# Output weights in rows of 3584 bytes, and the last sixteen value chunks summed and turned apart, in a one-core attention decode step

## The chip, the cores and the metric

The kernel runs on one core of one Trainium2 chip. The metric is device time in microseconds (us), from the start to the end of the program on that core; 653.36 us is the median of three runs before the change (653.25 to 653.43).

## What is computed

One token for each of four sequences (B = 4, D = 448) goes through a layer norm and then two branches. Branch A is attention over a cache; branch B is a small two-layer network with GELUs. The output adds their product to x.

```python
q = (xn @ wq).reshape(B, 1, 16, 256)              # 16 query heads of 256
k, v = repeat(k_cache, 2), repeat(v_cache, 2)     # 8 kv heads, 8192 positions, bf16
p = softmax(einsum("bhqd,bhkd->bhqk", q, k) / 16)
o = einsum("bhqk,bhkd->bhqd", p, v)
s = o.reshape(B, 1, 4096) @ wo                    # wo is [4096, 448]
out = x + s * silu(B(xn))                         # xn = layernorm(x)
```

The two caches are 128 MiB each. wq and wo are 3584 KB each; the other weights are smaller. Nearly all bytes are read once and used once.

## The kernel before

**Pairs.** The 32 (sequence, kv head) combinations are taken two at a time: 16 pairs, two neighbouring kv heads of one sequence. A pair's keys are two tiles of 4 MB (`kn`, one per kv head slot), its values 8 MB (`vb`). Partition p holds positions in chunks of 128 columns: `NC2` = 128 chunks of 128 positions for the pair, the upper 64 partitions for the second kv head.

**TensorE's program** (`prog_pe`) is written out by hand. `body` runs once for each pair. For every group of four key chunks it transposes eight 128x128 blocks (`f_t`, L655), VectorE and ScalarE copy them from PSUM to SBUF (`evac`, L350 and L352), and three groups later the score matmuls follow (`f_s`, L668). At the end of a pair, the value matmuls of the *pair before* stand between the last score groups (`f_pv`, L700): eight columns of probabilities `pT` are the weights, two value chunks (512 columns) stream through, and four matmuls write four groups of 32 PSUM partitions of `psv`. Then come the row maxima, a broadcast, and the exponentials on ScalarE (`exps`, L376).

**The turn.** `psv` holds sums by (group, chunk parity, head row) on partitions and by the 256 head columns along the free axis. VectorE copies it to `po` (`f_po`, L540). In the next pair's key stage `f_tr` (L693) multiplies `po`, every second column as weights, with a selector `sel`, in float32: this adds the groups up and puts head columns on the 128 partitions. VectorE multiplies with the reciprocal of the row sums into `OT_all` (`f_ot`, L543).

**After the last pair** `finish` does the rest: the turn of pair 14, the output matmuls of the heads whose wo rows are there early (`f_ou`, L736, four groups of 32 partitions, summed later by `selb` at L776), the values of pair 15 in pieces as they land, and the output matmuls of the other heads (`f_o`, L746, two halves of 224 columns side by side into `o_ps`). The pieces are bounded by `PIECES`. The last two (`ND = 2`) are not summed in `psv`: `f_direct` (L756) loads each chunk's every second column as weights and streams 32 columns of `pT` through, so that the result comes out turned at once in `ol_ps`; the turn of `po` (L783) is added into the same PSUM. VectorE's last `f_ot` writes pair 15's part of OT; after `f_o` it multiplies and adds (L590, L592), and two small stores end the program.

**Loads.** All large loads stand in SyncE's queue, in the order: wq, w3, keys of pair 0, w4, nine heads of wo (`dwo`), then keys of pair i and values of pair i-1 in turn, at the end the values of pair 15 in pieces into the key buffer (`dvl0` to `dvl4`), and last wo for heads 0 to 6 in four loads (`LATE`, `dwl0` to `dwl3`). Heads 0 to 6 come late because w4 lies in their place in `wo_sb` until the middle of the program (`v_w4`). A load into a used buffer waits for VectorE's release (`v_k`, `v_v`). A partition of a wo head holds two rows of 448: 1792 bytes in one run. `take` (L318) waits for a semaphore and takes its count off again.

Of the kernel before, what the change touches and what calls it, by code (L numbers as in the profile page):

```python
# [7 lines left out]
ALU = mybir.AluOpType  # L8
AX = mybir.AxisListType
F32 = dt.float32  # L10
BF16 = dt.bfloat16

P = 128
# [50 lines left out]
def bass_recurrent_scan__gqa_block_cached__mixer_s_mlp__decode_kernel(  # L64
# [13 lines left out]
    Bn, Sq, D = A_x.shape  # L78
    _, HKV, SK, DH = A_k_cache.shape
    HD = A_wq.shape[1]  # L80
    HQ = HD // DH
    REP = HQ // HKV
# [10 lines left out]
    NDG = 2  # L93
# [26 lines left out]
    PIECES = (0, 64, 96, 116, 124, NC2)  # L120
# [3 lines left out]
    ND = 2  # L124

    LATE = ((0, 1), (2, 3), (4, 5), (6,))
    NLATE = sum(len(g) for g in LATE)
# [16 lines left out]
    with ExitStack() as es:  # L144
        def sb(name, shape, dty):
            return es.enter_context(nc.sbuf_tensor(name, shape, dty))
# [5 lines left out]
        wo_sb = sb("wo_sb", [P, HQ, NHALF, D], BF16)  # L152
# [15 lines left out]
        po = sb("po", [P, CP * DH], F32)  # L168
        rmax = sb("rmax", [P, REP], F32)
# [42 lines left out]
        assert DK * HDH <= NCH * DH and NF <= NLATE * NHALF  # L212
# [13 lines left out]
        OT = OT_all[:, 2 * PW:].rearrange("p (b g d r) -> p g r d b", g=HKV, d=NHALF,  # L226
                                                 r=REP)
# [8 lines left out]
        def prog_sp(sp):  # L236
# [59 lines left out]
            wo_src = A_wo.rearrange("(h p c) n -> p h (c n)", p=P, c=NHALF)  # L296

            def load_wo(lo, hi, sem):
                sp.dma_start(wo_sb[:, lo:hi].rearrange("p h c n -> p h (c n)"),
                             wo_src[:, lo:hi]).then_inc(S[sem], 16)  # L300

            load_wo(NLATE, HQ, "dwo")
# [6 lines left out]
            for i, hs in enumerate(LATE):  # L309
                load_wo(hs[0], hs[-1] + 1, "dwl%d" % i)  # L310
# [6 lines left out]
        def take(eng, name, n=1):  # L317
            return eng.wait_ge(S[name], n).then_inc(S[name], -n)  # L318
# [75 lines left out]
        def prog_dve(v):  # L394
# [147 lines left out]
            def f_ot(at, src):  # L542
                return v.tensor_tensor(  # L543
                    OT_all[:, bass.ds(at, PW)].rearrange("p (s a r) -> p a s r", s=NS, a=NHALF),
                    src.rearrange("p a (s r) -> p a s r", s=NS),
                    rz[:, :].rearrange("p (s r) -> p s r", s=NS).unsqueeze(1).broadcast_to(
                        [P, NHALF, NS, REP]), ALU.mult)

            def turned(at):
                take(v, "p_m3")  # L550
                return f_ot(at, psm[:, P + 2 * NR:P + 2 * NR + NHALF * NR].rearrange(
                    "p (a n) -> p a n", a=NHALF))

            with nc.Fori(0, NH * TW, PW, engines=[mybir.EngineType.DVE]) as at:
# [32 lines left out]
            f_ot(NH * TW + PW, ol_ps[:, 0:NHALF * PVW].rearrange("p (a n) -> p a n", a=NHALF)[  # L587
                :, :, 0:NR]).then_inc(S["v_ot"], 1)
# [6 lines left out]
        def prog_pe(pe, xn_mark, xn2_mark):  # L595
# [91 lines left out]

            def f_tr():
                take(pe, "v_po")
                for dh in range(NHALF):  # L690
                    o = P + (2 + dh) * NR
                    for i in range(CP):
                        ins = pe.matmul(psm[:, o:o + NR], po[:, i * DH + dh:(i + 1) * DH:NHALF],  # L693
                                        sel[:, i, 0:NR], start=(i == 0), stop=(i == CP - 1))
                ins.then_inc(S["p_m3"], 1)
# [33 lines left out]
            ALONE = HQ - NS * REP  # L729

            def f_ou(hs):
                for hq in hs:
                    for dh in range(NHALF):
                        k = (hq - NLATE) * NHALF + dh
                        o = k % NCG * CGW
                        ins = pe.matmul(ou_ps[o:o + PQ, 0:D], OT[:, hq // REP, hq % REP, dh, :],  # L736
                                        wo_sb[:, hq, dh, :], start=(k < NCG),
                                        stop=(k >= (ALONE - NLATE) * NHALF - NCG))
                return ins


            def f_o(hs, stop=False):
                for hq in hs:
                    for dh in range(NHALF):
                        for i in range(NDG):
                            ins = pe.matmul(o_ps[i * PQ:(i + 1) * PQ, 0:DQ],  # L746
                                            OT[:, hq // REP, hq % REP, dh, :],
                                            wo_sb[:, hq, dh, i * DQ:(i + 1) * DQ], start=False,
                                            stop=stop and hq == hs[-1] and dh == NHALF - 1)
                return ins  # L750

            def f_direct(i):
                take(pe, "dvl%d" % i, 16)
                for dh in range(NHALF):
                    for kk in range(PIECES[i], PIECES[i + 1]):
                        ins = pe.matmul(ol_ps[:, dh * PVW:(dh + 1) * PVW], kv[:, kk, dh:DH:NHALF],  # L756
                                        pT[:, kk * NR:kk * NR + PVW],
                                        start=(dh == 0 and kk == PIECES[NPIECE - ND]),
                                        stop=(dh == NHALF - 1 and kk == NC2 - 1))
                return ins  # L760

            def finish():
                f_tr()
                take(pe, "dwo", 16)
                take(pe, "v_ot")
                f_ou(range(NLATE, ALONE)).then_inc(S["p_ou"], 1)
                take(pe, "a_exp")
                f_sum()
                pb = PIECES[NPIECE - ND]
                for i in range(NPIECE - ND):  # L770
                    take(pe, "dvl%d" % i, 16)
                    ins = f_pv(kv, PIECES[i], PIECES[i + 1], pb)
                    if i == 0:
                        take(pe, "v_a")
                        for n in range(NDG):
                            pe.matmul(o_ps[n * PQ:(n + 1) * PQ, 0:DQ], selb[:, :],  # L776
                                      ou_f[:, n * DQ:(n + 1) * DQ], start=True, stop=False)
                ins.then_inc(S["p_pv"], 1)
                f_direct(NPIECE - ND)
                take(pe, "v_po")  # L780
                for dh in range(NHALF):
                    for i in range(CP):
                        pe.matmul(ol_ps[:, dh * PVW:(dh + 1) * PVW],  # L783
                                  po[:, i * DH + dh:(i + 1) * DH:NHALF], sel[:, i, :],
                                  start=False, stop=False)
                f_direct(NPIECE - 1).then_inc(S["p_pv"], 1)
                take(pe, "dwl0", 16)
                f_o(LATE[0])
                take(pe, "v_ot")
                f_o(range(ALONE, HQ))  # L790
                for i in range(1, len(LATE)):
                    take(pe, "dwl%d" % i, 16)
                    ins = f_o(LATE[i], i == len(LATE) - 1)
                ins.then_inc(S["p_o"], 1)
# [65 lines left out]
```

## Time and profile before

| what | value |
|---|---|
| median of three runs | 653.36 us (653.25 to 653.43) |
| the profiled execution's own time | 652.84 us |
| its span, first to last instruction | 651.3 us |
| TensorE: matmul busy, weight load busy | 501.3 us (77%), 409.0 us (63%) |
| VectorE, ScalarE busy | 257.2 us (39%), 268.7 us (41%) |
| mean granted TensorE clock | 0.882 |
| DMA | 279.13 MB, mean 429 GB/s |
| DMA packets | 10642; 1029 under 512 bytes, 3081 under 2 KB |
| transposes of keys (L655) | 4096 matmuls, 301.6 us |
| the turn in `f_tr` (L693) | 136 passes, 258 ns each; loads of 128 columns in f32, 196 ns |
| wo matmuls at the end (L746) | 44, each 128x224, 267 ns |

PE is TensorE's matmuls, PEld its weight loads, which run beside them; a float32 matmul shows as two passes. "L318" is the line of the helper that waits for a semaphore, so a wait whose releaser is "PEq L318" is one on TensorE's own queue for some semaphore. "issue" is time for which the profile shows no cause. Times inside the span count from its start. Where the text names landings, it means the moment at which the last of the 16 DMA engines has counted up that load's semaphore.

### The profile page before, as it was taken

Reading aid. Unit: us, or ns where it says so; the run is one execution under the profiler, and the core shown is the slowest. Engines: PE = TensorE matmul, PEld = TensorE weight load, DVE = VectorE, ACT = ScalarE, POOL = GpSimd, SP = SyncE. Lnnn points to the kernel's source line nnn. Section 1 sums busy time; section 2 is a strip of 40 time slices with the busy share of each in tenths; the row PEclk is TensorE's granted clock in tenths of the full one; section 3 lists DMA queues with packets and bytes.
Section 4 is the critical chain, followed back from the end, with each engine's and each line's share of the span. In section 5 each row is a group of like instructions: output and inputs, shape, how many; then the busy total and the mean of one; then the engine's idle time right before and its main releaser. Section 6 shows DMA issues by size and latency. Waiting matters only on the chain. (4 is left out here: it accounts for less than half of the span.)

```text
span 651.3 us, 22030 instructions
## 1 busy us (share of the span) xinstructions
PE 501.3 (77%) x9695; PEld 409.0 (63%) x9695; DVE 257.2 (39%) x507; ACT 268.7 (41%) x361; POOL 3.7 (1%) x18
## 2 busy tenths in 40 slices
PE   2978979695876959589587967959597695959957
PEld 0976949384673938559286764928567393755924
DVE  7434525252452524335153442515245252433511
ACT  6644626063451615436144542606345161543600
POOL 2000000000000000000000000000000000000000
PEclk9989979697996969889788997969889797987968
DMA  9999999999999999999999999999999999999997
GB/s 382 436 419 436 431 437 447 421 441 429 442 443 407 455 415 447 423 431 459 411 452 415 455 423 429 441 427 443 425 445 435 417 449 421 445 425 429 455 406 305
DMA packets 10642, 279.13 MB, mean 429 GB/s; under 512 B 1029, under 2 KB 3081, under 8 KB 3593
## 3 DMA queue, kind: packets, MB, share of 16 engines
q1 hardware_dynamic: 10616, 278.99, 99.5%
q8 instruction: 7, 0.11, 0.1%
q14 instruction: 3, 0.02, 0.0%
q10 hardware_dynamic: 16, 0.01, 0.0%
HBM read 278.99 MB, written 0.00 MB: 428 GB/s over the span
## 5 line engine op out<-in xcount | busy, mean ns | idle before, releaser
L655 PE MATMUL pst<-ident_b,kn 128*128 128x128 bf16 x4096 | 301.6, 221 | 21.6 <-PEq L318 20.1
L352 ACT ACTIVATE kT<-pst 128x1024 bf16<-128x1024 bf16 x224 | 226.1, 1023 | 116.6 <-ACTq L318 116.2
L350 DVE COPY kT<-pst 128x1024 bf16<-128x1024 bf16 x288 | 197.5, 691 | 172.4 <-DVEq L318 172.4
L655 PEld LDWEIGHTS pst<-ident_b,kn 128*128 128x128 bf16 x4096 | 239.2, 99 | 23.5 <-issue 23.5
L700 PE MATMUL psv<-vb,pT 128*8 128x512 bf16 x1024 | 105.1, 506 | 99.6 <-PEq L318 98.7
L668 PE MATMUL psc<-qc,kT 128*128 128x4 bf16 x4096 | 174.2, 165 | 7.7 <-PEq L318 5.8
L668 PEld LDWEIGHTS psc<-qc,kT 128*128 128x128 bf16 x4096 | 153.4, 97 | 36.8 <-issue 36.5
L376 ACT ACTIVATE pT<-psc,negb 64x128 bf16<-64x128 f32 x64 | 28.4, 535 | 244.0 <-ACTq L318 243.8
L700 PEld LDWEIGHTS psv<-vb,pT 128*8 128x8 bf16 x1024 | 25.0, 94 | 133.2 <-issue 123.1
L511 DVE TENSOR_REDUCE rmax<-psc 64x2 f32<-64x256 f32 x32 | 13.5, 422 | 137.2 <-DVEq L318 137.0
L693 PE MATMUL psm<-sel,po 128*128 128x4 f32 x136 | 18.4, 258 | 1.4 <-PEq L318 1.4
L693 PEld LDWEIGHTS psm<-sel,po 128*128 128x128 f32 x136 | 17.3, 196 | 1.5 <-issue 1.5
L376 ACT ACTIVATION_READ_ACCUMULATOR pT<-psc,negb 64x1 f32 x64 | 16.4, 256 | 0.0
L540 DVE COPY po<-psv 128x512 f32<-128x512 f32 x17 | 11.7, 691 | 9.1 <-DVEq L318 9.1
L532 DVE COPY negb<-psm 128x4 f32<-128x4 f32 x16 | 2.6, 161 | 31.3 <-DVEq L318 31.3
L521 DVE TENSOR_REDUCE gmax<-psm 2x2 f32<-2x128 f32 x16 | 4.5, 279 | 21.2 <-DVEq L318 21.2
L364 ACT ACTIVATE vb<-pT 128x5000 bf16<-128x5000 bf16 (+2 forms) x3 | 10.6, 3568 | 0.1
L677 PEld LDWEIGHTS psm<-ident_f,rmax 128*2 128x2 f32 x16 | 1.3, 80 | 12.6 <-issue 12.6
L681 PEld LDWEIGHTS psm<-diag,ones_f 2*128 2x128 f32 x32 | 4.7, 182 | 7.0 <-issue 7.0
L600 PE MATMUL pst<-ident_b,xn_b 4*128 4x4 bf16 x14 | 0.7, 162 | 9.6 <-DVE xn_b L425 9.6
L600 PEld LDWEIGHTS pst<-ident_b,xn_b 4*128 4x128 bf16 x14 | 0.5, 100 | 10.5 <-issue 9.5
L685 PE MATMUL psw<-rowsum,ones_f 128*128 128x4 f32 x34 | 6.5, 263 | 0.0
(93 smaller groups left out, 86.4 us busy)
## 6 DMA issues: line engine op xcount, KB each, us to landing
kn<-in_A_k_cache_dram SPq DMA_DIRECT2D x30, 4096.0 KB, 26.5
kn<-in_A_k_cache_dram SPq DMA_DIRECT2D x4, 2048.0 KB, 16.7
vb<-in_A_v_cache_dram SPq DMA_DIRECT2D x2, 4096.0 KB, 23.1
kn<-in_A_v_cache_dram SPq DMA_DIRECT2D x1, 4096.0 KB, 27.7
vb<-in_A_wq_dram SPq DMA_DIRECT2D x1, 3584.0 KB, 11.4
kn<-in_A_v_cache_dram SPq DMA_DIRECT2D x1, 2048.0 KB, 26.2
wo_sb<-in_A_wo_dram SPq DMA_DIRECT2D x1, 2016.0 KB, 40.8
vb<-in_B_w_dram SPq DMA_DIRECT2D x1, 1568.0 KB, 14.1
```

The costliest lines, as they stand in the source:

```text
L350: engine.tensor_copy(dst, src).then_inc(S["v_ev"], 1)
L352: engine.activation(dst, src, ACT.Copy).then_inc(S["a_ev"], 1)
L364: f = act.activation(t, pT[:, 0:1].broadcast_to([P, t.shape[1]]), ACT.Copy)
L376: ins = act.activation(pT[own, 0:NC2 * NR].rearrange("p (c n) -> p n c", n=NR)[:, n], psc[own, 0:NC2 * NR].rearrange("p (c n) -> p n c", n ...
L511: ins = v.tensor_reduce(rmax[own, :], psc[own, 0:NC2 * NR].rearrange("p (c n) -> p n c", n=NR)[:, t * REP:(t + 1) * REP], AX.X, ALU.max)
L540: v.tensor_copy(po[:, :], psv[:, 0:CP * DH]).then_inc(S["v_po"], 1)
L655: ins = pe.transpose(dst[:, n * P:(n + 1) * P], kn[:, t, GC * j + kl, half * P:(half + 1) * P], ident_b[:, :])
L668: ins = pe.matmul(psc[:, kk * NR:(kk + 1) * NR], kT[:, j % RING, n * P:(n + 1) * P], qc[:, :, half, :], start=(half == 0), stop=(half == N ...
L681: pe.matmul(psm[:, P:P + NR], ones_f[0:REP, :], diag[:, :], start=True, stop=True).then_inc(S["p_m2"], 1)
L685: pe.matmul(psw[:, 0:NR], ones_f[:, :], rowsum[:, :], start=True, stop=True).then_inc(S["p_s"], 1)
L693: ins = pe.matmul(psm[:, o:o + NR], po[:, i * DH + dh:(i + 1) * DH:NHALF], sel[:, i, 0:NR], start=(i == 0), stop=(i == CP - 1))
L700: ins = pe.matmul(psv[o:o + CP * NR, 0:CP * DH], pT[:, kk * NR:(kk + CP) * NR], src[:, kk:kk + CP, :].rearrange("p c d -> p (c d)"), start ...
```

## The change

wo is laid out by kv head instead of by query head. A partition of a kv head's tile now holds four rows of wo, 3584 bytes in one run; the lower 64 partitions belong to the first query head of the kv head, the upper 64 to the second, and a partition's rows are four neighbouring columns of that head (`NDC` = 4). So the turn has to put every fourth head column on a partition, for each query head on its own half: `turn_out` makes four column steps x two halves, with 64 columns of weights each. `f_ot` runs once for each half. The first wo load has four kv heads (eight query heads), the late ones three whole kv heads and the fourth in two halves. The last three pieces of values (112 to 128, sixteen chunks) no longer go through `f_direct`: `f_end` sums them like the others but one chunk at a time, into `psc`; VectorE copies them to a new tile `pb`, and `pb` is turned after `po`, into the same PSUM. Output matmuls of late groups 0 and 1 now stand ahead of the wait for pair 15's OT (before: heads 0 and 1 alone).

```diff
-    PIECES = (0, 64, 96, 116, 124, NC2)
+    PIECES = (0, 64, 96, 112, 120, 124, NC2)
-    ND = 2
-    LATE = ((0, 1), (2, 3), (4, 5), (6,))
+    ND = 3
+    NDC = REP * NHALF
+    LATE = ((0, 0, NDC), (1, 0, NDC), (2, 0, NDC), (3, 0, NDC // 2), (3, NDC // 2, NDC))
...
-        wo_sb = sb("wo_sb", [P, HQ, NHALF, D], BF16)
+        wo_sb = sb("wo_sb", [P, HKV, NDC, D], BF16)
+        pb = sb("pb", [P, DH], F32)
...
-            wo_src = A_wo.rearrange("(h p c) n -> p h (c n)", p=P, c=NHALF)
-            load_wo(NLATE, HQ, "dwo")
+            wo_src = A_wo.rearrange("(g p c) n -> p g c n", p=P, c=NDC)
+            sp.dma_start(wo_sb[:, NLATE:].rearrange("p g c n -> p g (c n)"),
+                         wo_src[:, NLATE:].rearrange("p g c n -> p g (c n)")
+                         ).then_inc(S["dwo"], 16)
...
-            for i, hs in enumerate(LATE):
-                load_wo(hs[0], hs[-1] + 1, "dwl%d" % i)
+            for i, (g, lo, hi) in enumerate(LATE):
+                sp.dma_start(wo_sb[:, g, lo:hi].rearrange("p c n -> p (c n)"),
+                             wo_src[:, g, lo:hi].rearrange("p c n -> p (c n)")
+                             ).then_inc(S["dwl%d" % i], 16)
...
             def f_ot(at, src):
-                return v.tensor_tensor(
-                    OT_all[:, bass.ds(at, PW)].rearrange("p (s a r) -> p a s r", s=NS, a=NHALF),
...
+                for r in range(REP):
+                    own = slice(r * P // REP, (r + 1) * P // REP)
+                    ins = v.tensor_tensor(
+                        OT_all[own, bass.ds(at, PW)].rearrange("p (s c) -> p s c", s=NS),
+                        src[own].rearrange("p c (s r) -> p r s c", s=NS)[:, r],
+                        rz[own, :].rearrange("p (s r) -> p r s", s=NS)[:, r].unsqueeze(2)
+                        .broadcast_to([P // REP, NS, NDC]), ALU.mult)
+                return ins
...
             take(v, "p_pv")
             f_po()
             take(v, "p_pv")
+            v.tensor_copy(pb[:, :], psc[:, 0:DH]).then_inc(S["v_po"], 1)
+            take(v, "p_pv")
+            f_ot(NH * TW + PW, ol_ps[:, 0:NDC * NR].rearrange("p (c n) -> p c n", c=NDC)).then_inc(S["v_ot"], 1)
...
+            def turn_out(dst, src, n, start, stop):
+                for c in range(NDC):
+                    for i in range(n):
+                        for r in range(REP):
+                            own = slice(r * P // REP, (r + 1) * P // REP)
+                            ins = pe.matmul(dst[own, c * NR:(c + 1) * NR],
+                                            src[:, i * DH + c:(i + 1) * DH:NDC], sel[:, i, 0:NR],
+                                            start=start(c, i), stop=stop(c, i))
+                return ins
...
-            def f_direct(i):
+            def f_end(i):
                 take(pe, "dvl%d" % i, 16)
-                for dh in range(NHALF):
-                    for kk in range(PIECES[i], PIECES[i + 1]):
-                        ins = pe.matmul(ol_ps[:, dh * PVW:(dh + 1) * PVW], kv[:, kk, dh:DH:NHALF],
-                                        pT[:, kk * NR:kk * NR + PVW],
...
+                for kk in range(PIECES[i], PIECES[i + 1]):
+                    o = kk % NCG * CGW
+                    ins = pe.matmul(psc[o:o + NR, 0:DH], pT[:, kk * NR:(kk + 1) * NR], kv[:, kk, :],
+                                    start=(kk < PIECES[NPIECE - ND] + NCG), stop=(kk >= NC2 - NCG))
                 return ins
...
                 ins.then_inc(S["p_pv"], 1)
-                f_direct(NPIECE - ND)
+                f_end(NPIECE - ND)
                 take(pe, "v_po")
-                for dh in range(NHALF):
-                    for i in range(CP):
-                        pe.matmul(ol_ps[:, dh * PVW:(dh + 1) * PVW],
-                                  po[:, i * DH + dh:(i + 1) * DH:NHALF], sel[:, i, :],
-                                  start=False, stop=False)
-                f_direct(NPIECE - 1).then_inc(S["p_pv"], 1)
-                take(pe, "dwl0", 16)
-                f_o(LATE[0])
+                turn_out(ol_ps, po, CP, lambda c, i: c == 0 and i == 0, lambda c, i: False)
+                for i in range(NPIECE - ND + 1, NPIECE):
+                    ins = f_end(i)
+                ins.then_inc(S["p_pv"], 1)
+                take(pe, "v_po")
+                turn_out(ol_ps, pb, 1, lambda c, i: False, lambda c, i: c == NDC - 1
+                         ).then_inc(S["p_pv"], 1)
+                last = len(LATE) - 1
+                for i in range(2):
+                    take(pe, "dwl%d" % i, 16)
+                    f_o(*LATE[i])
                 take(pe, "v_ot")
-                f_o(range(ALONE, HQ))
-                for i in range(1, len(LATE)):
+                for g in range(ALONE, HKV):
+                    f_o(g, 0, NDC)
+                for i in range(2, len(LATE)):
                     take(pe, "dwl%d" % i, 16)
-                    ins = f_o(LATE[i], i == len(LATE) - 1)
+                    ins = f_o(*LATE[i], stop=i == last)
                 ins.then_inc(S["p_o"], 1)
```

`f_tr` calls `turn_out` as well, so the turn in every pair's key stage has the new form. The line numbers of the kernel after differ: the turn is L699, `f_o` L754, `f_end` L763.

## The prediction

> **What bounds the kernel now.** I read the page's slices and queues first, then the chain that ended last, then the last microseconds in order of time, then the DMA issues. Slices and queue (each DMA digit is the busy share of 16 engines in tenths):
>
> ```profile
> PEclk9989979697996969889788997969889797987968
> DMA  9999999999999999999999999999999999999997
> GB/s 382 436 419 436 431 437 447 421 441 429 442 443 407 455 415 447 423 431 459 411 452 415 455 423 429 441 427 443 425 445 435 417 449 421 445 425 429 455 406 305
> ...
> q1 hardware_dynamic: 10616, 278.99, 99.5%
> ```
>
> One queue moves 279 MB without a hole. The landing marks say the same: every 4 MB takes 9.65 to 9.71 us (two exceptions of 9.84 and 9.95), that is 433.7 GB/s. The issues are far ahead: the last value pieces and the wo loads stand 25 to 28 us in the queue before they land, so no issue and no buffer release is late.
>
> ```profile
> 647.95 0.04 issue
> 647.99 0.98 PE pst L746 x12
> 649.00 0.40 DVE res L590
> 649.42 0.38 DVE out_b L592
> ```
>
> This is the chain of waits (start, length, what). It begins where TensorE waits for the third late wo load. The order of time (start, length, engine, line, idle before), and then the issues of late wo (KB each, us from issue to landing):
>
> ```profile
> 643.65 0.69 DVE L540 COPY po<-psv 128x512 f32<-128x512 f32 x1 [5.26 <-DVEq L318]
> 644.46 1.02 PEld L783 LDWEIGHTS pst<-sel,po 128*128 128x128 f32 x8
> 645.71 1.90 PE L746 MATMUL pst<-wo_sb,OT_all 128*32 128x224 bf16 x32
> 647.96 0.78 PEld L746 LDWEIGHTS pst<-wo_sb,OT_all 128*32 128x32 bf16 x12 [0.57 <-issue]
> ```
>
> ```profile
> wo_sb<-in_A_wo_dram SPq DMA_DIRECT2D x3, 448.0 KB, 27.1
> wo_sb<-in_A_wo_dram SPq DMA_DIRECT2D x1, 224.0 KB, 16.7
> ```
>
> The last load lands at 648.41, its four matmuls end at 648.96, VectorE and the store take the rest to 651.3. So the end is the DMA stream plus 2.9 us. But TensorE idles only 0.57 us between 645.7 and 648.96: it is a close second.
>
> Landings of the tail before: value pieces 634.63, 639.50, 642.55, 643.80, 644.45; late wo 645.58, 646.71, 647.86, 648.41.
>
> [...]448 KB of wo takes 1.13 us, where its bytes at 433.7 GB/s take 1.06. [...] The f32 loads of 128 columns start 117.5 ns apart (L783)[...]. [...]637.1 to 640.5 ran at clock 0.50. [...]at L736 four loads of 32 columns for four tiles start within 42 ns, and a tile's next load comes 38 to 42 ns after its own first.
>
> **The change, part by part: the stream.** Fixed cost of a packet, from landings: the first wo load took 4.97 us for 4.76 us of bytes, 0.21 over 73 packets an engine (with the semaphore's) = 3 ns; the late ones 3.96 for 3.70, 0.26 over 60 = 4.3 ns. The records' own durations give more (1792 bytes 74 ns, 2048 84, 4096 159: about 9 ns fixed). Before, wo is 72 + 56 = 128 row packets an engine; after, 32 + 24 of 3584 bytes and 16 of 1792 = 72. One more value piece adds 8 packets, two more DMAs add 2 semaphore writes: 46 fewer. At 3 to 4.3 ns that is -0.14 to -0.20 us, at 9 ns -0.41; nothing if the rows are cut to 1792 again. I take -0.16. It arrives in two parts: the first wo load carries eight heads for nine and ends 0.64 us earlier, so all later landings come 0.64 earlier, and late wo is 0.44 longer, pieces 0.04. New landings: third piece 641.31, then 642.56, 643.21, 643.86; late wo 644.96, 646.06, 647.16, 647.71, 648.26. SyncE issues two DMAs more (0.43 each), hidden by the 16.7 us in which the last one waits[...].
>
> **The loop.** The turn of the sums (L693) is 4 f32 matmuls, 8 passes of 128 columns; it becomes 16, 32 passes of 64 columns in two column tiles. [...] If both tiles load together, 32 passes take 16 x 64 = 1.03 us, as the 8 do now (1.02); if not, 2.06. I take together, by L736. Even 2.06 costs nothing here: it stands in the key stage, after which TensorE waits up to 7.5 us for values (the L700 wait), and the key and value loads are issued 10 us and more ahead. Without that cover 1 us x 16 = 16 us. VectorE's second multiply (0.15) is covered by its waits for the queue (172 us at L350).
>
> **The finish, on TensorE.** This is where cost can appear; all follows data 0.64 us earlier.
> 1. Turn of pair 14: starts 633.70, ends 635.02 (1.03 + 0.29 latency), two multiplies to 635.47, then f_ou with 8 matmuls for 10 (two rounds of 0.19, not three), the row sum, and the first value matmuls at 636.42 (before 636.94).
> 2. Pieces 0 and 1 run to about 641.3; piece 2 lands 641.31, its 8 matmuls end 642.05 (0.11 to the first load, 0.03 to the matmul, 0.22 to the second round, 0.38 for its last). Wait and copy to po 0.15 + 0.69, TensorE takes it at 643.0. Piece 3 (8 matmuls of 256 columns, 4 side by side, some 0.45) fits in between.
> 3. Turn of po, 32 passes: to 644.15 with its start. Pieces 4 and 5: to 644.65. This sum now needs a second copy, psc to pb, which was not there: 0.15 wait + 0.43 (128x512 takes 691 ns, 448 625, so 1.03 ns an element: 256 gives 427) + 0.12. TensorE stands in that wait from 644.4 to 645.35, with the wo matmuls whose data has landed queued behind it; VectorE has nothing else to do then.
> 4. Turn of pb, 16 passes: 0.52, result at 646.15; two multiplies, OT at TensorE 646.7. Meanwhile late wo groups 0 and 1 (16 matmuls, a pair per 96 ns as now: 0.8) to 646.8; groups 6 and 7 to 647.6; group 2 to 648.05; half of 3 to 648.3; the last half landed at 648.26, four matmuls 0.55: **648.84**.
> By the stream alone: 648.26 + 0.55 = 648.81. A tie, against 648.96. [...] The removed direct turn (24 matmuls 0.90, po 1.10) is inside these steps.
>
> Both ends of the sum: -0.41 (9 ns a packet[...]) and +1.9 (serial loads, below). The profiled execution took 652.84, 1.5 more than its span; the median of the runs is 0.5 above it, and I carry the difference over: 653.36 + 0.05 = 653.4.
>
> **Rivals.**
> *Loads of the two tiles do not overlap* (slower). The turns then take 2.06, 2.06 and 1.03 us. Step 1 ends 1 us later, pieces 0 and 1 at 642.3 (the cold window until 640.5 included), po is ready at 643.65, its turn ends 645.7, pb at 646.95, its turn 648.0, and the wo matmuls behind it (0.85 + 0.77 + 0.45 + 0.25 + 0.5) bring 650.85: +1.9 us, 655.3. For: no 64-column f32 load is in this trace; weights step 16 bytes where the old step is 8 (117 ns against 109 for the contiguous L685). Against: L736, and L643, where f32 loads of two tiles start 4 ns apart. It decides over the stream from about 34 ns a pass, and passes the bound of 0.2% from about 55. A cold window at 643.9 does the same by another way: the window 633.7 to 637.1 had TensorE busy for 2.26 us, half of it passes of 4 moving columns, and the next was cold, while 2.08 us of mostly wide matmuls (640.5 to 643.9) kept the clock. The new finish has more narrow passes and the wait for pb; half clock over 3.4 us costs up to 1.7: 655.0.
> *The stream gains more*: 9 ns a packet and TensorE not late: 652.9. Against: the landings give 3 to 4.3.
> *The rows are cut at 1792 after all*: no packet saved, ten packets added (+0.04), finish as forecast: 653.5.
>
> **How the numbers follow.** Forecast 653.4 (own range 653.0 to 654.0) 0.58; TensorE the bound 0.27 (654.2 to 655.6, three quarters of it over 654.67); more from the stream 0.08; no longer rows 0.07. The bound of telling is 0.2%, 1.3 us, about what a measurement can tell from no change. Faster by that would need more than all packet overhead that the landings show (0.47 us): 0.02. Slower 0.2, within 0.78. The range runs from the stream's gain, 652.8, into the second case, 655.2.
>
> **What would show it.** Packets fewer by about 740 and the last wo landing 0.1 to 0.3 us earlier: the stream. The turn's 32 loads taking about 1.05 us: the overlap; 2.1 the first rival. The last four wo matmuls starting right after their landing: the stream still bounds; wo matmuls without a gap from the pb turn to the end: TensorE does. A 0.50 clock after 643.9 names the cold window. I am wrong if [...]a key stage grows enough to hold up a load.

## The result, and the profile after

The changed kernel takes 669.14 us (median of six runs, 665.58 to 670.77); the kernel before took 653.16 beside it (six runs, 652.89 to 653.43). The ratio is 1.0237, with a 95% interval of 1.021 to 1.0265. The forecast was 653.4, with a range up to 655.2: the change is 2.4% slower, far outside it.

The profiled execution took 668.94 us with a span of 667.3, against 652.84 and 651.3 before: 16.0 us more span. Two numbers divide them. The last wo load lands at 660.57, where it landed at 648.41: 12.2 us are lost in the stream. The last wo matmul ends at 664.96, that is 4.4 us behind that landing, where it was 0.55: 3.8 us are lost after the stream.

**The stream has a hole.** These are slices and queues of the page of the changed kernel (before: every DMA digit but the last was 9, and q1 stood at 99.5%):

```profile
PEclk9789878797988879798659997879899687989968
DMA  9999999999999999999994999989999999999995
GB/s 388 430 428 430 438 452 434 409 444 430 446 418 448 442 414 458 407 442 424 448 432 190 397 440 411 466 383 442 437 440 440 411 469 401 420 438 442 440 412 203
...
q1 hardware_dynamic: 9880, 278.99, 97.3%
q8 instruction: 16, 0.26, 0.1%
```

The second GB/s value behind the middle is 190 where its neighbours are above 390, and the DMA digit there is 4. q1's share fell by 2.2 points although it moves the same 278.99 MB. q8, which the page calls "instruction", moves 16 KB at a time. In the profile before it had 7 transfers and it now has 16; nine of the sixteen start between 334 and 378 us.

TensorE in order of time around the middle, just after the small network's second layer (`mlp`, the last L648 line) in the changed kernel (start, length, engine, line, operation, count, idle before):

```profile
326.03 1.65 PE L643 MATMUL psv<-wo_sb,hT 128*4 128x448 bf16 x14 [1.87 <-PEq L319]
328.69 0.96 PE L648 MATMUL psw<-ou_f,selb 128*32 128x224 f32 x4 [1.01 <-PEq L319]
345.21 3.57 PE L660 MATMUL pst<-ident_b,kn 128*128 128x128 bf16 x32 [15.55 <-PEq L319]
```

TensorE is idle for 15.55 us. Nothing that it waits for is late; it stands in two branches. In the trace, the branch at L812 (the `If` that skips `finish` in the first half of the outer loop) lasts 7.97 us from 328.74, and the one at L807 (back to the head of the outer loop) lasts 7.75 us from 336.86. Before, the same two lasted 0.33 and 0.22. The first of the nine instruction transfers starts 5.6 us after the first of these branches began. One of the nine lies in the first branch and two in the second, and each branch ends 1.4 to 1.5 us after the last transfer in it. Some 20 us later the stream runs dry, because the key buffers were given back late: the first key load behind the middle is issued at 359.32, where it was issued at 339.80 before. Changed kernel by stretches of 2 us (clock, DMA share and GB/s are the last three columns):

```profile
core 0: us, PE busy (x) PEld busy (x) DVE busy (x) ACT busy (x) POOL busy (x), PEclk, DMA share, GB/s
350.00:352.00 2.00, 2.00 (x53) 2.00 (x51) 1.36 (x2) 1.08 (x2) 0.00 (x0) 1.00 0.61 262
352.00:354.00 2.00, 2.00 (x41) 1.98 (x39) 0.71 (x2) 0.97 (x1) 0.00 (x0) 1.00 0.04 8
354.00:356.00 2.00, 2.00 (x46) 1.98 (x45) 0.00 (x0) 0.66 (x1) 0.00 (x0) 1.00 0.00 0
356.00:358.00 2.00, 2.00 (x53) 2.00 (x51) 1.62 (x4) 1.46 (x3) 0.00 (x0) 1.00 0.03 8
358.00:360.00 2.00, 1.78 (x48) 1.67 (x45) 1.34 (x3) 0.95 (x1) 0.00 (x0) 1.00 0.00 0
360.00:362.00 2.00, 1.91 (x39) 1.94 (x40) 0.75 (x2) 0.53 (x1) 0.00 (x0) 1.00 0.91 279
```

TensorE is working at full clock again here, and no data moves for almost 8 us. Three landings carry the loss: 354.74, 372.60 and 384.70 come 20.26, 17.86 and 12.10 us behind the one before them, for a steady 19.32, 9.67 and 9.67. That is 11.6 of the 12.2 us.

**The finish trails the stream.** The changed kernel's last 11 us in order of time, of which I show the last sums and what follows from them:

```profile
656.02 0.69 DVE L541 COPY po<-psv 128x512 f32<-128x512 f32 x1 [3.89 <-DVEq L319]
...
656.86 2.08 PE L699 MATMUL pst<-sel,po 128*64 128x4 f32 x32 [0.79 <-PEq L319]
...
658.87 0.39 PE L763 MATMUL psc<-kn,pT 128*4 128x256 bf16 x8
...
659.42 0.42 DVE L591 COPY pb<-psc 128x256 f32<-128x256 f32 x1 [2.72 <-DVEq L319]
...
660.00 1.12 PE L699 MATMUL pst<-sel,pb 128*64 128x4 f32 x16 [0.73 <-PEq L319]
...
661.05 3.91 PE L754 MATMUL pst<-wo_sb,OT_all 128*32 128x224 bf16 x48
```

A turn of 32 passes takes 2.08 us, not 1.03; the turn of `pb` 1.12, not 0.52. Then 48 wo matmuls take 3.91 us. All of them stand behind the turn of `pb`, although the first of their data had landed more than 3 us earlier (the five land from 657.49 to 660.57). The granted clock was 0.50 from 646.94 to 653.76 and again from 660.59 to 664.00: the wo matmuls begin at half clock, and the last 16 of the 48 start after it. The chain of waits (start, length, what) of the changed kernel, and then its late wo issues (KB each, median us from issue to landing):

```profile
660.00 1.12 PE pst L699 x16
661.12 3.86 PE pst L754 x47
664.98 0.02 issue
665.00 0.39 DVE res L595
665.40 0.02 issue
665.42 0.38 DVE out_b L597
```

```profile
wo_sb<-in_A_wo_dram SPq DMA_DIRECT2D x3, 448.0 KB, 24.3
...
wo_sb<-in_A_wo_dram SPq DMA_DIRECT2D x2, 224.0 KB, 21.1
```

Before, the chain began with a matmul that waited for a wo load. Now no load is in it: it is TensorE's own work without a gap, from the `pb` turn to the end. And the issues aren't what is late: the loads stood in the queue for 21 and 24 us.

### The profile page after: what moved, and what is told of

Same layout as the page of the kernel before. It is cut to its first block, busy times and chain, and to the rows that moved or that the text cites. A ratio compares the mean times of both kernels' runs of the same rounds, so it can differ in the third digit from the quotient of the medians.

```text
span 667.3 us, 22951 instructions
## 1 busy us (share of the span) xinstructions
PE 532.4 (80%) x10135; PEld 439.5 (66%) x10135; DVE 260.7 (39%) x526; ACT 268.5 (40%) x361; POOL 3.7 (1%) x18
## 2 busy tenths in 40 slices
DMA packets 9914, 279.28 MB, mean 419 GB/s; under 512 B 1060, under 2 KB 1320, under 8 KB 2856
## 3 DMA queue, kind: packets, MB, share of 16 engines
q1 hardware_dynamic: 9880, 278.99, 97.3%
HBM read 278.99 MB, written 0.00 MB: 418 GB/s over the span
## 5 line engine op out<-in xcount | busy, mean ns | idle before, releaser
L660 PE MATMUL pst<-ident_b,kn 128*128 128x128 bf16 x4096 | 310.6, 225 | 35.0 <-PEq L319 33.5
L660 PEld LDWEIGHTS pst<-ident_b,kn 128*128 128x128 bf16 x4096 | 244.5, 100 | 37.1 <-issue 36.9
L673 PEld LDWEIGHTS psc<-qc,kT 128*128 128x128 bf16 x4096 | 155.8, 98 | 37.8 <-issue 37.2
L699 PE MATMUL psm<-sel,po 128*64 128x4 f32 x544 | 35.5, 262 | 1.4 <-PEq L319 1.4
L699 PEld LDWEIGHTS psm<-sel,po 128*64 128x64 f32 x544 | 34.0, 215 | 1.8 <-issue 1.5
## 6 DMA issues: line engine op xcount, KB each, us to landing
vb<-in_A_wq_dram SPq DMA_DIRECT2D x1, 3584.0 KB, 11.6
```

Source lines behind the costliest of these rows:

```text
L660: ins = pe.transpose(dst[:, n * P:(n + 1) * P], kn[:, t, GC * j + kl, half * P:(half + 1) * P], ident_b[:, :])
L673: ins = pe.matmul(psc[:, kk * NR:(kk + 1) * NR], kT[:, j % RING, n * P:(n + 1) * P], qc[:, :, half, :], start=(half == 0), stop=(half == N ...
L699: ins = pe.matmul(dst[own, c * NR:(c + 1) * NR], src[:, i * DH + c:(i + 1) * DH:NDC], sel[:, i, 0:NR], start=start(c, i), stop=stop(c, i))
```

## The experiments

At first there were two theories for the hole. Theory A: TensorE's program has grown, so that on the way around the outer loop the code it jumps to has to be fetched, behind a full DMA stream. Theory B: the turn, twice as long as forecast (2.09 us), holds up the key stage. For the finish: the 64-column loads do not overlap between tiles, or each load takes longer; and how much of the rest is the clock.

### The loop heads moved: e1_heads_moved

```diff
-            with nc.Fori(0, 2, engines=[e], head_slot={e: 64}) as part:
-                with nc.Fori(0, NPAIR // 2, engines=[e], head_slot={e: 88}):
+            with nc.Fori(0, 2, engines=[e], head_slot={e: 0}) as part:
+                with nc.Fori(0, NPAIR // 2, engines=[e], head_slot={e: 24}):
```

This is the changed kernel; only the place of the two loop heads in TensorE's code differs, 64 instructions earlier.

> The kernel after, with the two loop heads of TensorE's program placed 64 instruction slots earlier (outer 64 to 0, inner 88 to 24); no instruction differs. Theory A (TensorE's outer loop, some 1,850 instructions from its head to its back edge, no longer stays on chip, so the jump back after the middle section refetches it): the two branches of 8 us shrink to about 0.3 us, the DMA hole of 11.5 us at 345 to 385 us goes, and the time is 657 to 658 us. Theory B (the longer turn in every key stage releases key buffers late): nothing changes, 667 to 670 us. In both, the last wo matmul still ends some 4 us after the last wo load has landed.

Measured: 658.95 us (657.33 to 659.99, four runs), ratio to before 1.0097 (1.0081 to 1.0114). The same place in order of time as above, for this kernel:

```profile
328.23 0.96 PE L648 MATMUL psw<-ou_f,selb 128*32 128x224 f32 x4 [1.02 <-PEq L319]
329.58 3.11 PE L660 MATMUL pst<-ident_b,kn 128*128 128x128 bf16 x32 [0.39 <-PEq L319]
```

The idle time is 0.39 us for 15.55. The two branches take 0.34 and 0.22 us, the page counts 8 instruction transfers, and the last wo load lands at 648.37. So 10 us of the 16 come from the place of the code, with every operation the same. The finish's loss stays: 4.33 us of wo matmuls, all of them behind the last landing.

### The same move in the kernel before: e2_before_heads_moved

```diff
-            with nc.Fori(0, 2, engines=[e], head_slot={e: 64}) as part:
-                with nc.Fori(0, NPAIR // 2, engines=[e], head_slot={e: 88}):
+            with nc.Fori(0, 2, engines=[e], head_slot={e: 180}) as part:
+                with nc.Fori(0, NPAIR // 2, engines=[e], head_slot={e: 204}):
```

> The kernel before, with both loop heads 116 slots later (outer 64 to 180, inner 88 to 204); same instructions, same work. [...] Theory A: two long branches after the middle section, a DMA hole of about 11 us, 662 to 666 us. Theory B: no change, 653.0 to 653.4 us.

Measured: 668.41 us (666.71 to 668.91, four runs), ratio 1.024 (1.0223 to 1.0257). In order of time, for this kernel:

```profile
327.70 0.57 PE L643 MATMUL psw<-ou_f,selb 128*32 128x224 f32 x4 [1.01 <-PEq L318]
343.71 2.83 PE L655 MATMUL pst<-ident_b,kn 128*128 128x128 bf16 x25 [15.44 <-PEq L318]
350.62 0.91 PE L655 MATMUL pst<-ident_b,kn 128*128 128x128 bf16 x7 [4.08 <-issue]
```

The kernel before, moved by 116 instructions, has the hole of the changed one: 15.44 us idle, branches of 6.88 and 8.26 us, 16 instruction transfers, three late landings (20.60, 19.71 and 11.42 us), the last wo load at 662.11. It cost more than the 662 to 666 us expected. The landings slipped by 13.7 us, and the last line shows a third pause: 4.08 us among the transposes of keys, for which the trace has no wait, with an instruction transfer from 348.46. Moving the code takes the hole out of one kernel and puts it into the other: theory A is shown in both directions.

### The turn done twice: e3_before_turn_twice

```diff
-                for dh in range(NHALF):
-                    o = P + (2 + dh) * NR
...
+                for again in range(2):
+                    for dh in range(NHALF):
+                        o = P + (2 + dh) * NR
...
```

The kernel before, with the whole turn in `f_tr` repeated; the second one computes the same sums once more.

> The kernel before, with the turn of the sums done twice over (the second pass writes the same values): about 2.0 us of TensorE for each key stage, as in the kernel after, with 32 instructions more in all. Theory A: no hole, 653.0 to 653.8 us. Theory B: key buffers late as in the kernel after, 660 us and more.

Measured: 653.61 us (652.64 to 655.45, twelve runs) against 652.90, ratio 1.0013 (1.0004 to 1.0022). The groups of this kernel (busy us, mean ns of one; idle before):

```profile
L694 PE MATMUL psm<-sel,po 128*128 128x4 f32 x272 | 34.6, 259 | 1.4 <-PEq L318 1.4
```

Each of the 17 turns now occupies TensorE for about 2.03 us (34.6 in all), as in the changed kernel, and there is no hole: the two branches take 0.33 and 0.22 us, the page counts 7 instruction transfers. Some 17 us of extra matmul work cost 0.7. That is the median: six of the twelve executions took 654.0 to 655.5, and the profile, of one that took 652.99, doesn't show why. A hole of 11 us is in none of them. Theory B falls.

### What a 64-column load costs: e4_load_forms and g1_load_step

Both are the kernel before with twelve extra f32 matmuls behind each turn, whose results nobody reads. They differ in the columns' distance and in the column tile (e4):

```diff
+                for n, (step, tiles) in enumerate(((4, (0, 0)), (4, (0, 1)), (1, (0, 1)))):
+                    for k in range(2):
+                        for t in tiles:
+                            own = slice(t * P // 2, (t + 1) * P // 2)
+                            ins = pe.matmul(psm[own, 256 + 8 * n + 4 * k:260 + 8 * n + 4 * k],
+                                            po[:, k:k + 64 * step:step], sel[:, 0, 0:NR],
+                                            start=True, stop=True)
```

g1 has `((1, (0, 0)), (2, (0, 0)), (4, (0, 0)))` in the first line.

> The kernel before, with twelve more float32 matmuls behind each turn, into unused PSUM: weights of 64 columns (i) with a step of 4 elements, all in the lower column tile, (ii) with a step of 4, lower and upper tile in turn, as in the kernel after, (iii) with a step of 1, in turn. Forecast's reading (tiles load together[...]): (i) 64 ns from load to load, (ii) and (iii) 32 ns. Reading C (tiles share one loader, 60 ns a load): (i), (ii) and (iii) 60 ns. Reading D (tiles load together but a load takes as long as one of 128 columns): (i) 120 ns, (ii) 60 ns; if the step is what costs, (iii) is faster than (ii).

> The kernel before with twelve extra f32 matmuls of 64 columns after each turn, all in one column tile, whose results nobody reads: four with neighbouring columns, four with columns 8 bytes apart, four with columns 16 bytes apart. If the distance sets the time of a load: about 57 ns a pass for the neighbours (twice the 28 ns seen with two tiles), 60 to 65 at 8 bytes, 120 at 16. If the alternation of tiles made the short time: all three alike. The time stays within 0.2% of before.

e4 took 653.67 us and g1 653.61, one run each. Distance from the start of one load to the next in the trace, steady part:

| load of 64 f32 columns | step | tiles | ns from load to load |
|---|---|---|---|
| g1 | 4 bytes | one | 55 to 59 |
| g1 | 8 bytes | one | 59 to 61 |
| g1 | 16 bytes | one | 118 to 121 |
| e4 | 4 bytes | two in turn | 27 to 29 |
| e4 | 16 bytes | two in turn | 60 on average (50, 70, 27, 93) |

Two tiles do load side by side: the distance halves with two tiles at either step. But with a step of 16 bytes one load takes as long, 120 ns, as 128 columns do at 8 bytes (117.5 ns, L783 before). In four of the seventeen stages of g1 half clock began within the run of 8-byte loads: these went from 60 to 107 ns, the 16-byte ones stayed at 119.

### The finish outside the loop, then its two losses: f1 to f4 and g2

```diff
-                with pe.If(part == 1):
-                    finish()
+            finish()
```

f1 is the changed kernel with the heads where they were and `finish` behind the outer loop, where no branch has to skip it.

> The kernel after, with the finish placed behind TensorE's outer loop instead of in a branch of its second round; loop heads as in the kernel after, the same work in the same order. The outer loop is then some 1,400 instructions long[...]. Theory A (refetch of the loop): no long branch, no DMA hole, the last wo load lands at 648.2 to 648.5 us, time as with the heads moved, 657 to 660 us.

Measured: 657.03 us (656.35 to 658.4, four runs) against 652.98; ratio 1.0054 (1.0038 to 1.0071). No long branch, 7 instruction transfers, last wo load at 648.36. TensorE's finish in f1 in order of time, and its clock by stretches (third column from the right):

```profile
644.42 2.09 PE L699 MATMUL pst<-sel,po 128*64 128x4 f32 x32 [0.79 <-PEq L319]
...
647.77 1.12 PE L699 MATMUL pst<-sel,pb 128*64 128x4 f32 x16 [0.73 <-PEq L319]
648.83 4.32 PE L754 MATMUL pst<-wo_sb,OT_all 128*32 128x224 bf16 x48
```

```profile
core 0: us, PE busy (x) PEld busy (x) DVE busy (x) ACT busy (x) POOL busy (x), PEclk, DMA share, GB/s
646.00:648.00 2.00, 1.26 (x21) 0.78 (x22) 0.42 (x1) 0.00 (x0) 0.00 (x0) 0.50 0.43 164
648.00:650.00 2.00, 2.00 (x30) 1.87 (x30) 0.33 (x2) 0.00 (x0) 0.00 (x0) 0.50 0.00 0
650.00:652.00 2.00, 2.00 (x24) 1.77 (x22) 0.00 (x0) 0.00 (x0) 0.00 (x0) 0.50 0.00 0
```

With the stream where it was forecast, the finish is as slow as in the changed kernel: 2.09 and 1.12 for the turns, and the first 42 of the 48 wo matmuls at clock 0.50 (to 652.62).

f2 is f1 with the same turn reading neighbouring columns. VectorE, which copies the sums to SBUF anyway, reads every fourth column of them in PSUM and so writes them in the order in which the turn reads them:

```diff
-                v.tensor_copy(po[:, :], psv[:, 0:CP * DH]).then_inc(S["v_po"], 1)
+                v.tensor_copy(po[:, :].rearrange("p (i c m) -> p i c m", i=CP, c=NDC),
+                              psv[:, 0:CP * DH].rearrange("p (i m c) -> p i c m", i=CP, c=NDC)
+                              ).then_inc(S["v_po"], 1)
...
-                                            src[:, i * DH + c:(i + 1) * DH:NDC], sel[:, i, 0:NR],
+                                            src[:, i * DH + c * DH // NDC:i * DH + (c + 1) * DH // NDC], sel[:, i, 0:NR],
```

`pb` is written likewise.

> The kernel with the finish outside, and VectorE writes po and pb in the order in which the turn reads them, so that the 64 weights of a pass lie side by side. If the step of 16 bytes made a load of 64 columns as long as one of 128: 32 passes take about 1.0 us instead of 2.03, 16 about 0.55, and the time falls by 1.5 to 2.5 us to 655.5 to 657.5; more, down to 653, if the finish thereby stays at full clock. If the two column tiles share one loader: no change.

Measured: 654.0 us (652.56 to 655.32, twelve runs), ratio 1.0009 (1.0 to 1.0018): 3.0 us below f1. In order of time, f2:

```profile
642.87 1.10 PE L702 MATMUL pst<-sel,po 128*64 128x4 f32 x32
...
645.03 0.64 PE L702 MATMUL pst<-sel,pb 128*64 128x4 f32 x16 [0.73 <-PEq L319]
645.59 2.39 PE L757 MATMUL pst<-wo_sb,OT_all 128*32 128x224 bf16 x23
648.81 2.64 PE L757 MATMUL pst<-wo_sb,OT_all 128*32 128x224 bf16 x25 [0.82 <-issue]
```

The turns take 1.10 and 0.64 us, close to the forecast's 1.03 and 0.52. VectorE's copies take 0.69 and 0.42, as in f1: reading every fourth column cost no time here. The wo matmuls still run at half clock (from 645.74 in this trace, which is of the slowest of the twelve executions). The gap of 0.82 us is no wait for data: it falls between two matmuls of a head group that came early, and TensorE takes the semaphores of the last three loads only behind it. An instruction transfer starts at 646.41, so it may be a fetch again; that was not shown.

f3 is f1, and f4 is f2, with 40 wide matmuls that nobody reads in waits of the finish:

```diff
+            def warm(n):
+                for k in range(n):
+                    o = k % NCG * CGW
+                    pe.matmul(pst[2][o:o + 8, 0:512], ident_b[:, 0:8],
+                              vv[:, 2 * k:2 * k + 2, :].rearrange("p c d -> p (c d)"),
+                              start=True, stop=True)
...
+                warm(12)
                 f_tr()
+                warm(12)
...
                 f_end(NPIECE - ND)
+                warm(8)
                 take(pe, "v_po")
...
                 ins.then_inc(S["p_pv"], 1)
+                warm(8)
                 take(pe, "v_po")
```

> The kernel with the finish outside, and 40 wide matmuls into unused PSUM in the four waits of the finish (12, 12, 8, 8), added work that nobody reads. If half clock costs the finish its last 2 us: no 0.50 window after 640 us, a pair of wo matmuls every 96 ns instead of 187, the 48 in some 2.4 us instead of 4.3, and 655.5 to 657 us. If the clock has another cause or the wo matmuls wait for something else: no change, or slower by the added work, 659 to 661 us.

> Both changes together: contiguous weights in the turn and the wide matmuls in the waits. If the two causes are all of the lost time in the finish, TensorE ends with the stream as was forecast: 652.7 to 653.6 us. If something else costs more, 654 us and above.

f3: 656.38 us (653.88 to 658.14, eleven runs), ratio 1.0048 (1.0037 to 1.0059). f4: 655.17 (652.32 to 658.4, twenty runs), ratio 1.0021 (1.0007 to 1.0034). Neither median says that the clock matters. f3's trace fell to half clock all the same, at 645.65, so f3 doesn't test what the clock costs:

```profile
643.34 2.09 PE L699 MATMUL pst<-sel,po 128*64 128x4 f32 x32
...
647.56 4.69 PE L754 MATMUL pst<-wo_sb,OT_all 128*32 128x224 bf16 x48
```

f4's twenty times lie in two groups, nine from 652.32 to 653.01 and eleven from 655.16 to 658.4, with none between. Its profiled execution (656.14) belongs to the second, and its clock fell to 0.50 at 644.55, 2.5 us ahead of 48 wo matmuls that took 4.58 us. The 3.4 us ahead of that hold a wait of 1.0 us for a value piece and most of a turn, whose passes are four columns wide. So g2 is f4 with 28 more such matmuls, in the waits ahead of value pieces 2 and 3:

```diff
                 for i in range(NPIECE - ND):
+                    if i == 2:
+                        warm(16)
                     take(pe, "dvl%d" % i, 16)
...
+                warm(12)
                 f_end(NPIECE - ND)
```

> Contiguous turn, finish behind the loop, and added wide matmuls that nobody reads in all waits of the finish (28 more than the kernel with 40 of them). If the slow half of that kernel's executions is a window of 3.4 us that starts late in the finish after a thinly used one: nearly all executions near 652.5 (652.3 to 653.2), clock 1.0 from 641 to the end. If the clock has other causes, the two groups at 652.5 and 655 to 658 stay as they were.

Measured: 652.7 us (652.47 to 653.39, thirteen runs) against 653.04, ratio 0.9994 (0.9986 to 1.0002). The slower group is gone. In order of time, and by stretches, g2:

```profile
643.04 0.60 PE L773 MATMUL pst<-vb,ident_b 128*8 128x512 bf16 x8
643.58 1.10 PE L702 MATMUL pst<-sel,po 128*64 128x4 f32 x32
644.61 0.39 PE L766 MATMUL psc<-kn,pT 128*4 128x256 bf16 x8
644.83 0.60 PE L773 MATMUL pst<-vb,ident_b 128*8 128x512 bf16 x8
645.73 0.64 PE L702 MATMUL pst<-sel,pb 128*64 128x4 f32 x16 [0.30 <-PEq L319]
646.30 2.52 PE L757 MATMUL pst<-wo_sb,OT_all 128*32 128x224 bf16 x48
```

```profile
644.00:646.00 2.00, 1.70 (x50) 1.18 (x48) 0.42 (x1) 0.00 (x0) 0.00 (x0) 1.00 1.02 409
646.00:648.00 2.00, 2.00 (x49) 1.98 (x48) 0.33 (x2) 0.00 (x0) 0.00 (x0) 1.00 0.41 153
648.00:650.00 2.00, 0.82 (x18) 0.60 (x14) 0.77 (x2) 0.00 (x0) 0.00 (x0) 1.00 0.00 0
```

The clock is 1.0, and the wo matmuls take 2.52 us for f1's 4.32 and f4's 4.58. The last one ends at 648.82, 0.55 us after the last landing at 648.27: the stream is the end again. The 28 matmuls also move the code behind them, but a fetch isn't what they took away: f4's one profile has no pause in the finish without a wait. g2 is the fastest form of the change, but the interval of its ratio holds 1, so it isn't shown to beat the kernel before.

### e1 once more: g3_heads_moved_again

> The changed kernel with the loop heads moved, once more, beside its neighbours on one chip. If the 1.9 us between it (658.95) and the kernel with the finish behind the loop (657.03) came from the chip or from the windows of the clock: 656.5 to 658.5 with a wide spread. If the place of the finish costs: 658.5 to 660 again.

Measured: 659.42 us (656.89 to 659.92, four runs), ratio 1.0083 (1.0065 to 1.0101). So it is slower than f1, but the trace doesn't put that in the finish. At 18 us the first branch at the outer loop's head lasts 6.4 us (5.8 in e1; in f1 no branch lasts over 0.5 us), and the landings after it, 53.82, 59.93 and 66.63, come 10.29, 6.12 and 6.70 us apart for 9.70, 4.84 and 4.84 in the profile before. In the profiled execution 3 us are lost there for good: the last wo load lands at 651.49. Moving the heads mends the middle and costs something at the start; f1 is the cleaner proof. Why e1's own profiled execution lost less at the start (0.74 us) was not followed up.

## Why the prediction was wrong

**The sum.** By medians: 669.14 to 657.03 (f1) is 12.1 us for the code's place; to 654.0 (f2) 3.0 for the distance of the columns; to 652.7 (g2) 1.3 for the clock. That accounts for all of the distance to the forecast of 653.4. The last two shares aren't clean. From f1 to f2 the two turns became only 1.5 us shorter (2.09 to 1.10 and 1.12 to 0.64); the rest of the 3.0 must lie in executions of f2 that have no profile, and the clock may have a part in it. And where f4's profiled execution lost its clock, its last wo matmul ended 2.8 us later than g2's (651.63 for 648.82).

**The loop: the step that failed.** The prediction priced 24 added passes per turn by their duration and found them covered. The durations are covered: even 2.06 us, which it allowed, costs 0.7 us over all 17 turns (e3). What it left out is that the passes are also instructions. A pass is a load and a matmul, so `body` holds 48 more, and by my count of the program `finish` 115 more. The skip of `finish` and the way back to the loop head then took 7.97 and 7.75 us, with instruction transfers inside both, for 0.33 and 0.22 us before. So I read them as waits for code that was not at hand. Going around `body` alone didn't bring them on: it has more than 1,200 instructions by my count, and in the changed kernel nearly seven passes of it, from 60 to 322 us, brought no new transfer.

Where the hole begins can be counted in the programs. As the place of the outer loop's jump back I take its head's `head_slot` and add the instructions from the head to the jump. That is about 1,403 in f1, 1,690 before, 1,722 in e3, 1,786 in e4 and g1 and 1,789 in e1, all without the hole; it is 1,806 in e2 and 1,853 in the changed kernel, which have it. (The 1,850 in e1's expectation is this place.) The count can be a few instructions off. So among these programs the hole begins between 1,789 and 1,806. e4 and g1 say that it isn't `body` alone: theirs has the same 48 more. Why it begins there was not shown, nor why six of the nine transfers come only after the two branches, from 348 to 378 us.

**The price of such a stall in a stream that never pauses.** The prediction said that issues are far ahead, 10 us and more. That was so: before, the first key load behind the middle was issued at 339.80, 14.5 us ahead of the landing of the load in front of it. In the changed kernel it was issued at 359.32, 4.6 us behind that landing (354.74). The 15.6 us stop and some delay around it had used the lead up, and 11.6 us came back as missing data.

**The finish: its estimate of one load failed, not its overlap.** The step took 64 ns for a load of 64 columns, which was its author's estimate (the trace before has none; its loads of 128 columns at 8 bytes start 117.5 ns apart), and two tiles side by side, 32 ns a pass. Side by side is right (e4, and f2's 32 passes take 1.10 us). The load is 120 ns at 16 bytes (g1), 60 a pass. The first rival forecast 2.06 us for a turn, with the opposite reason: its number was measured (2.08), its mechanism not, and so the 2.1 us that the prediction set as its sign could not tell the two apart. The prediction had even named the sign, 117 ns at 8 bytes against 109 for neighbours, and used it only as a point against itself; the distance doubles it only at the next step.

**The cold window.** The rivals named it ("half clock over 3.4 us costs up to 1.7") and took it as an alternative to slow loads. It came with them. In f1 both hit, the clock for 1.8 us on the wo matmuls alone; f1's 657.03 is above the range without any hole, and the prices that the prediction had for the two, 1.9 and 1.7 us, come to 657.0 if both are added to its 653.4. That the turns of four moving columns bring the half clock on is my reading, not shown (last section).

**The stream: right.** Landings, forecast against f1, which has no hole (us; forecast on the time axis of the profile before):

| load | before | forecast | f1 |
|---|---|---|---|
| first wo load, time it took | 4.97 | 4.33 | 4.30 |
| value piece 2 | 642.55 | 641.31 | 641.15 |
| last value piece | 644.45 | 643.86 | 644.06 |
| late wo, first | 645.58 | 644.96 | 645.13 |
| late wo, last | 648.41 | 648.26 | 648.36 |

Packets fell from 10642 to 9914, by 728 for the forecast 740; those of q1 alone by 736. Most of what the first load gained was given back by the larger late ones, as forecast. The rivals "the stream gains more" and "the rows are cut at 1792" are out.

**The rest of the finish: right once its two terms are.** In g2, where the loads are short and the clock full, the last wo matmul ends at 648.82; the prediction has 648.84. TensorE's wo matmuls run there without a gap to the end, and they end 0.55 us behind the last landing: the tie that was forecast. The 0.05 us that it adds to the old time rests on its author's estimate for going between 32 and 64 columns of weights, which no run measured apart.

## What to carry to other kernels

An added instruction has a duration and a place. When a loop written out by hand grows, count the instructions between its head and every taken branch, and look at the instruction queue's transfers and the branches' own durations in the trace: a move of 116 instructions cost 2.4% here with the same operations (e2), and one of 64 gave back 1.5% (e1). Price a weight load by the distance of its columns as well as their number (64 f32 columns took 60 ns at 8 bytes and 120 at 16, g1), and let the engine that copies anyway put them side by side (its copy took 0.69 us either way, f1 and f2). A slower narrow step can be charged again on the wide work behind it: in f1, behind the slow turns, the 48 wo matmuls took 4.32 us with the clock at 0.50 for most of them, for 2.52 at 1.0 in g2.

## What was not expected of the hardware

- Two taken branches of TensorE lasted 7.97 and 7.75 us in the changed kernel, with instruction transfers inside them, and 6.88 and 8.26 in e2, while the packet record of a 16 KB instruction transfer in the changed kernel shows 0.88 to 1.42 us; the same branches took 0.33 and 0.22 us before, with no transfer inside them.
- In g1 a 64-column f32 load took 57 ns with a step of 4 bytes, 60 with 8, 120 with 16. At half clock the 8-byte load took 107, the 16-byte one still 119.
- VectorE's copy of 128x512 f32 out of PSUM took 0.69 us whether it read the columns in order (f1) or every fourth one (f2); it wrote in order in both.
- TensorE counts as busy in passes of four moving columns, but they did not keep the clock up: in f1 it was idle for only 0.8 of the 3.4 us ahead of 645.79, 1.4 us of which were a turn, and half clock followed (whole stretches of equal clock in these traces last 3.41 us or a multiple of it). f3 says it more sharply: idle for 0.35 of the 3.4 us ahead of 645.65, 2.1 us of which were a turn, and half clock followed. Before, TensorE was idle for 1.35 of the 3.4 us ahead of 643.94, with no turn among them, and full clock followed. That the narrow passes count for little is what I read from this; no run varied them alone, and the runs show only that wide matmuls in the waits kept the clock (g2).
